# GpSimd's long instructions cut in two, and a new order of all engines' queues, in a fused attention and feed-forward kernel

## The chip, the cores and the metric

The kernel runs on one core of one Trainium2 chip. A core has five engines that work side by side and meet only at semaphores: PE (matrix products), DVE (vector work), ACT (scalar functions), POOL (GpSimd, slower vector work, and some DMA issues), and SP, which here issues DMAs. Each engine takes the instructions of its own queue strictly in order. The metric is the device time of one execution in microseconds; smaller is better.

## What is computed

Attention in which some heads see all earlier keys and the others only four "sink" keys and a window of 64, followed by a feed-forward layer with the nonlinearity h - tanh(h):

```python
scores = scale * np.matmul(q, k.transpose(0, 1, 3, 2))      # 4 x 8 heads, 768 x 768, head size 64
stream_keep = causal & (is_sink | in_win)                   # n_sink = 4, window = 64
mask = np.where(is_retrieval[head], causal, stream_keep)    # 3 of 8 heads see everything
a = softmax(np.where(mask, scores, -1e9))
x = np.matmul(a, v)                                         # as (3072, 512)
h = x @ w_in                                                # (512, 2048)
out = ((h - np.tanh(h)) @ w_out).astype(np.float32)         # (2048, 512)
```

## The kernel before

The 3072 tokens are worked on in 12 tiles of 256, three tiles for each of the four sequences. The work on one tile goes through these stages, which the kernel's operations carry as names:

- q, k and v are loaded. For tile 0 (load_first) and tile 1 (load_cast) q and k are transposed by PE. Tile 1's q and k arrive packed two rows to a partition in the buffer t16p and are copied into t16 in halves (line 714 onward, table IE says by which engine), then transposed (st_T) and copied into QK (table TE). From tile 3 on, gather copies the heads into another order: DVE works out the order of the heads (by_rank, result perm_i, L1163), POOL reads it into registers and copies q, k (L854) and v (L890) head by head, and SP issues the transposes as DMAs (turn, L756).
- st_S forms scores (PE L1373), ACT takes the exponential into pt or ptn (L1392), DVE multiplies by a mask (L1405 to L1429). st_A multiplies by v (PE L1457); keys that are far away use vf, a copy of v multiplied by each head's flag: scale_v (POOL L946) for the first two tiles, spread for the others (L909, the sink copies L918, L929). DVE normalises (L1477, L1503, L1518) and the result reaches xT by transposes.
- H_unit multiplies by w_in (PE L1604), eight pairs of 128-wide chunks for each tile; ACT takes tanh (L1618) and DVE forms h - tanh(h) in gt (L1629).
- The second product: tiles 0 to 3 use O_group (PE L1677). Tiles 4 to 11 use a seven-product scheme on 2 x 2 blocks: DVE once forms four sums of blocks of w_out (L1717), and for every tile `sums` forms four sums S of blocks of gt, each in two halves of four chunks (L1770), so eight sums of 512 columns a tile. `piece` does the seven products (PE L1803), and `take`, `fold` and `add` (L1842, L1862, L1874) put them together in PSUM evacuations on ACT, DVE or POOL. For the last tile finale_b does so in its own order. Stores go out by SP and ACT (L1663, L1894).

No engine order is found at run time. The program first lists 1653 operations, numbered as they are made, and then issues them in the order of a list of numbers, SEQ; what an engine's queue holds is the part of SEQ that belongs to it. BANK says which PSUM bank each product uses, and SIZE how many times each warm-up matmul (L2144, numbers from 128) is repeated; these fill stretches at the start in which PE would otherwise be idle. Tables of letters (A is ACT, D is DVE, P is POOL) say which engine takes an operation that more than one can do: CASTS, TE, XE, IE, OE, SUMS (eight letters a tile), ADDS, TAKES. A branch at the end repeats the work in a general form if more than three heads see everything; it is not taken here.

The numbers that matter below: 37 and 38 are the first loads of v, 57 and 58 tile 1's loads of q and k (POOL's queue); 59 and 60 are the copies of tile 1's q halves, 61 and 62 those of k; 93 is the exponential of the last head pair of tile 0; 161 is tile 1's first scores; 170 is the mask of tile 1's second head pair; 244 is perm_i; 482 and 497 are stores of early tiles and 266 to 271 the loads of tile 4 (SP); 909 to 915 are tile 4's sums; 948 is a mask on ptn in tile 7 and 952 the product that uses it; 1615 to 1622 are the last tile's sums, 1636 an add there, 1642 and 1644 the last evacuations into the output block F, 1643 and 1645 its stores.

Of the kernel before, what the change touches and what calls it, by code (L numbers as in the profile page):

```python
# [16 lines left out]

SEQ = [
# [107 lines left out]
SIZE = {128: 19, 129: 14, 130: 10, 131: 6, 132: 3, 133: 4, 134: 3}  # L126
# [262 lines left out]
def kernel(  # L389
# [12 lines left out]
    nc = tc.nc  # L402
# [1920 lines left out]
```

## Time and profile before

| | us |
|---|---|
| three runs | 225.25, 222.69, 223.52 |
| their median | 223.52 |
| the profiled execution | 224.28 |
| its span, first to last instruction | 222.5 |
| granted clock of TensorE, mean over the span | 0.998 |
| DMA queue of SP and ACT loads, share of the span of 16 engines | 58.3% |
| DMA queue of POOL's loads, the same | 30.3% |
| POOL's L1770 (the sums) | 18 instructions, medians of their three groups 1.15 to 1.16 us |

The profile is one execution taken by the hardware profiler. "PE busy" has modelled ends, since matmuls are pipelined. In rows of the timeline the columns are the start, the time, the engine, the line of the kernel, the operation, what it writes and reads with partitions x columns, the count, and in brackets the idle time before it and what ended that. In rows of groups the columns after the bar are total busy us, mean ns of one, and the idle time before with what ended it. In rows of stretches they are, after the stretch and its length, the busy time and count of PE, PEld (weight loads), DVE, ACT and POOL, then the granted clock, the DMA share and GB/s.

### The profile page before, as it was taken

How to read it: one execution, taken by the hardware profiler on the slowest of the kernel's cores; microseconds unless marked ns; L12 is line 12 of the kernel's file. 1: busy time of each engine (PE TensorE's matmuls, PEld its weight loads, DVE VectorE, ACT ScalarE, POOL GpSimd, SP SyncE). 2: the span in 40 equal slices, each digit the busy share in tenths (PEclk: the TensorE clock that was granted, in tenths of full speed). 3: DMA queues.
4: the chain of work that ended last, by engine and by line, in shares of the span. 5: the costliest groups of instructions: out<-in, count | busy, mean ns of one | idle time of the engine just before them, and what ended most of it. 6: DMA issues, size and time to landing. Idle time of an engine off the chain costs nothing.

```text
span 222.5 us, 6576 instructions
## 1 busy us (share of the span) xinstructions
PE 211.9 (95%) x2474; PEld 175.5 (79%) x2474; DVE 182.0 (82%) x468; ACT 135.0 (61%) x216; POOL 128.4 (58%) x262
## 2 busy tenths in 40 slices
PE   7969999999999999999989999999999999999990
PEld 7657788778985585968877988988889888988870
DVE  5779889476878598979999888999899786799771
ACT  3979646897275759465557759473646857356110
POOL 8785967533784571578981873774864455034400
PEclk9999999999999999999999999999999999999999
DMA  6999999997999999899989499999246031010223
GB/s 171 170 200 198 198 160 160 182 190 165 228 188 205 233 187 236 169 198 236 253 167 189 100 175 225 252 196 174 73 78 164 0 94 52 21 29 0 99 94 105
DMA packets 112743, 34.56 MB, mean 155 GB/s; under 512 B 98882, under 2 KB 112194, under 8 KB 112706
## 3 DMA queue, kind: packets, MB, share of 16 engines
q1 hardware_dynamic: 86896, 26.75, 58.3%
q0 software_dynamic: 24992, 6.82, 30.3%
q10 hardware_dynamic: 818, 0.52, 0.8%
q8 instruction: 20, 0.33, 0.6%
q14 instruction: 17, 0.14, 0.2%
HBM read 27.26 MB, written 6.29 MB: 151 GB/s over the span
## 4 chain that ended last, share of the span: by engine, by line
PE 83%; DVE 7%; DMA 4%; issue 2%; POOL 2%; ACT 1%; POOLq 0%; DVEq 0%; ACTq 0%
PE banks L1604 35%; PE banks L1803 20%; PE banks L1677 13%; PE banks L1373 7%; PE banks L1457 7%; DMA t16p<-in_k_dram 3%; DVE gt L1629 1%; DVE m L1770 1%; POOL v L673 1%; DVE ptn L1405 1%; DMA out_dram<-ot 1%; PE banks L1248 1%; DVE gu L1874 1%; DVE ot L1862 1%; DVE pt L1429 1%
## 5 line engine op out<-in xcount | busy, mean ns | idle before, releaser
L1604 PE MATMUL banks<-xT,win 128*128 128x256 f16 x768 | 95.5, 273 | 0.2 <-DVE ot L1862 0.2
L1618 ACT ACTIVATE th<-banks 128x512 f32<-128x512 f32 x96 | 54.7, 599 | 48.3 <-PE banks L1604 37.9
L1604 PEld LDWEIGHTS <-win 128*128 128x128 f16 x768 | 72.5, 98 | 10.1 <-issue 1.0
L1629 DVE SCALAR_TENSOR_TENSOR gt<-th,banks 128x512 f16<-128x512 f32 x88 | 58.1, 679 | 7.8 <-ACT th L1618 6.8
L1392 ACT ACTIVATE pt<-banks 128x1024 f16<-128x1024 f32 (+3 forms) x57 | 49.3, 905 | 13.1 <-PE banks L1373 12.1
L854 POOL CAST t<-rawqk 128x256 f16 x64 | 24.7, 412 | 17.0 <-DMA rawqk<-in_q_dram 9.1
L1803 PEld LDWEIGHTS <-m 128*128 128x128 f16 x256 | 24.4, 98 | 3.3 <-issue 0.4
L1677 PE MATMUL banks<-wout,gt 128*128 128x256 f16 (+1 forms) x160 | 25.7, 294 | 0.0
L890 POOL CAST v<-rawv 128x128 f16 x64 | 19.5, 333 | 8.0 <-DMA rawv<-in_v_dram 7.9
L1503 DVE TENSOR_TENSOR x16t<-banks,rinv 128x128 f32 (+1 forms) x80 | 22.8, 286 | 1.3
L1373 PE MATMUL banks<-QK 64*128 64x128 f16 (+1 forms) x343 | 20.8, 236 | 0.0
L1803 PEld LDWEIGHTS <-gt 128*128 128x128 f16 x192 | 18.3, 98 | 2.4 <-issue 0.3
L1373 PEld LDWEIGHTS <-QK 64*128 64x128 f16 x343 | 13.0, 94 | 7.3 <-issue 6.0
L1770 POOL TENSOR_TENSOR m<-gt 128x512 f16<-128x512 f16 x8 | 9.3, 1158 | 16.3 <-ACT th L1618 10.9
L1457 PEld LDWEIGHTS <-pt 128*128 128x128 f16 x390 | 16.1, 97 | 2.3 <-issue 1.2
L1392 ACT ACTIVATE ptn<-banks 128x1024 f16<-128x1024 f32 (+1 forms) x18 | 17.1, 952 | 1.1 <-PE banks L1373 1.0
L1677 PEld LDWEIGHTS <-gt 128*128 128x128 f16 x160 | 14.1, 98 | 4.6 <-issue 0.7
L1803 PE MATMUL banks<-wout,gt 128*128 128x256 f16 x128 | 17.7, 273 | 0.0
L1803 PE MATMUL banks<-wout,m 128*128 128x256 f16 x128 | 17.6, 273 | 0.0
L1457 PE MATMUL banks<-v,pt 128*128 128x65 f16 x208 | 16.0, 193 | 0.0
L1429 DVE TENSOR_TENSOR pt<-pt,m4r 128x1024 f16<-128x1024 f16 (+1 forms) x18 | 13.2, 733 | 2.7 <-ACT pt L1392 2.7
L1457 PE MATMUL banks<-vf,pt 128*128 128x65 f16 x182 | 13.0, 193 | 0.7 <-DVE gt L1629 0.7
(129 smaller groups left out, 309.7 us busy)
## 6 DMA issues: line engine op xcount, KB each, us to landing
rawqk<-in_q_dram SPq DMA_DIRECT2D x18, 256.0 KB, 4.3
out_dram<-ot SPq DMA_DIRECT2D x18, 256.0 KB, 2.8
rawqk<-in_k_dram SPq DMA_DIRECT2D x17, 256.0 KB, 4.2
rawv<-in_v_dram SPq DMA_DIRECT2D x16, 256.0 KB, 4.9
win<-in_moe_w_in_dram POOLq DMA_DIRECT2D x4, 512.0 KB, 8.9
wout<-in_moe_w_out_dram POOLq DMA_DIRECT2D x4, 512.0 KB, 8.4
out_dram<-ot SPq DMA_DIRECT2D x10, 128.0 KB, 3.7
v<-in_v_dram POOLq DMA_DIRECT2D x6, 128.0 KB, 7.2
```

The costliest lines, as they stand in the source:

```text
L854: nc.gpsimd.tensor_copy(out=c5()[:, :, :, s_ : s_ + 1, :], in_=r5()[:, :, :, at, :])
L890: nc.gpsimd.tensor_copy(out=v1s[b]()[:, g * NB : g * NB + NB, RANK[s_] : RANK[s_] + 1, 0:D], in_=rw()[:, :, at, :],)
L1373: nc.tensor.matmul(out=flat[:, 512 * hh + o : 512 * hh + o + nb * 128], lhsT=lhsT, rhs=QK[p_, hp, q_0 : q_0 + nb * 128], start=not added, ...
L1392: nc.scalar.activation(out=o_, in_=i_, func=AF.Exp, scale=inv_sqrt_d)
L1429: nc.vector.tensor_mul(out=pv, in0=pv, in1=m)
L1457: nc.tensor.matmul(out=av()[:, i, hh, :], lhsT=pt()[:, hh, co : co + 128], rhs=vv, start=(jb == first_jb[hh]), stop=(jb == qb),)
L1503: nc.vector.tensor_mul(out=xt()[:, :, at, :], in0=av()[:, :, hh : hh + 1, 0:D], in1=rinv()[:, :, hh : hh + 1].unsqueeze(3).to_broadcast([1 ...
L1604: nc.tensor.matmul(out=ph()[:, j, :], lhsT=w_in_t[fb // 4][:, cb, f0 : f0 + 128], rhs=xT()[:, :, cb, :], start=(cb == 0), stop=(cb == HP - 1),
L1618: lambda: nc.scalar.activation(out=th()[:], in_=ph()[:], func=AF.Tanh, scale=1.0 / XS),
L1629: nc.vector.scalar_tensor_tensor(out=o_, in0=a, scalar=-XS, in1=b, op0=ALU.mult, op1=ALU.add,)
L1677: nc.tensor.matmul(out=po()[:, c0:c1], lhsT=gt()[:, f, ts * 128 : ts * 128 + 128], rhs=w_out_t[:, f, c0:c1], start=(f == 0), stop=(f == NF ...
L1803: nc.tensor.matmul(out=po()[:, at : at + CM], lhsT=lhs(c), rhs=rhs(c), start=c == 0, stop=c == NC - 1,)
```

## The change

HALVES is 2, and a new helper, `parts`, cuts a range in two where the engine is POOL and leaves it whole otherwise. Three operations use it: the sums (two chunks of 128 columns each instead of four), the far products of scale_v (four heads each instead of eight) and the sink copies of spread (two of the four blocks each). Both halves belong to one operation of the list: the second follows the first directly on POOL's queue, and those who wait for the operation wait for the second.

SEQ, BANK, SIZE and the tables of engines are replaced. SUMS has 18 P before and 30 after; three sums go from POOL to DVE and fifteen the other way. Of ADDS, seven go from DVE to POOL and six back. Of the copies and evacuations in CASTS, TE, XE, IE, OE and TAKES, 23 change between ACT and DVE. The set of operations, what they compute and what they wait for stay.

In POOL's queue the loads at the start go from 37, 38, 57, 58 to 58, 37, 38, 57. In ACT's queue 60, 93 becomes 60, 59, 93. In DVE's queue 170 stands before 278, 174 and 175 instead of behind 174 and 175; 244 stands behind the shrink of tile 1's sixth pair (371) instead of behind 380 and 243; 948 no longer follows 914, which is POOL's; 1620 stands before 1622 and 1621, and 1617, 1605, 1612 and 1636 are POOL's. In PE's queue 981 stands ahead of 952. In SP's queue 482 and 497 stand ahead of 271 and 268.

```diff
+HALVES = 2
 SEQ = [
-    1, 4, 7, 8, 3, 5, 6, 14, 13, 10, 18, 0, 19, 9, 12, 11, 128, 20, 21, 22, 30, 31, 129, 51, 15, 35, 37,
...
+    311, 317, 307, 319, 265, 318, 320, 322, 314, 313, 482, 497, 271, 268, 507, 349, 508, 350, 361, 509,
...
+    1646, 1647, 1610, 1611, 1612, 1635, 1639, 1644, 1613, 1631, 1632, 1628, 1636, 1645, 1642, 1643,
+    1648, 1650, 1649, 1651, 1652,
 ]
...
-SIZE = {128: 19, 129: 14, 130: 10, 131: 6, 132: 3, 133: 4, 134: 3}
+SIZE = {128: 20, 129: 22, 130: 6, 131: 4}
...
+    def parts(eng, a, b):
+        n = HALVES if eng == "POOL" else 1
+        return [slice(a + (b - a) * i // n, a + (b - a) * (i + 1) // n) for i in range(n)]
...
-    TE = (('DA', 'AD', 'AD', 'DD'), ('AA', 'AA', 'AA', 'DD'), ('AD', 'DD', 'DD', 'AA'))
-    XE = ('DDAD', 'DAAD', 'DADA')
+    TE = (('AA', 'AA', 'DD', 'AA'), ('AA', 'DD', 'AA', 'DD'), ('AA', 'AA', 'DD', 'DA'))
+    XE = ('AADD', 'DAAD', 'DADA')
...
-    CASTS = ('DA', 'AA')
+    CASTS = ('DD', 'AD')
...
-    SUMS = ('DDDDDDDD', 'DDDDDDDD', 'DDDDDDDD', 'DDDDDDDD', 'DPDPDPPD', 'PDDDPDDD', 'DDDDDDDD', 'DDPDDDDD', 'DDDDDPPP', 'DPPDDDPD', 'DPDDDDPP', 'PDDDDDPD')
-    ADDS = ('PPP', 'PPP', 'PPP', 'PPP', 'DDD', 'DPP', 'PDP', 'PPP', 'PDP', 'DPD', 'PDD', 'DPP')
-    TAKES = ('AA', 'AA', 'AA', 'AA', 'AA', 'AA', 'AA', 'AA', 'AD', 'AA', 'AA', 'AA')
+    SUMS = ('DDDDDDDD', 'DDDDDDDD', 'DDDDDDDD', 'DDDDDDDD', 'DDDPPPPP', 'DDDDPDDD', 'DPPDDDPP', 'DDPPDDDP', 'PDPDPPPP', 'PPPDDDDP', 'PPDDDDPP', 'PDPDDDPD')
+    ADDS = ('PPP', 'PPP', 'PPP', 'PPP', 'DDP', 'PDD', 'PDD', 'PDP', 'DPD', 'PPD', 'PPP', 'PPP')
+    TAKES = ('AA', 'AA', 'AA', 'AA', 'AA', 'AA', 'AD', 'AA', 'AD', 'AD', 'AA', 'AA')
...
-    IE = (('DA', 'DA'), ('DA', 'DA'))
+    IE = (('AA', 'DD'), ('DA', 'DA'))
...
-    OE = ('AADA', 'DDDA', 'AAAA', 'AAAA', 'AAAA', 'AAAA', 'AAAA')
+    OE = ('AAAD', 'DADA', 'AAAA', 'AAAA', 'AAAA', 'AAAA', 'AAAA')
...
-                    lambda: nc.gpsimd.tensor_copy(
-                        out=vfs[b]()[0:64, :, NGEN:H, :],
...
+                    lambda: [
+                        nc.gpsimd.tensor_copy(
+                            out=vfs[b]()[0:64, x, NGEN:H, :],
...
+                        for x in parts("POOL", 0, 4)
+                    ],
...
-                    lambda jb=jb, fl=fl, eng=eng: engs[eng].tensor_mul(
-                        out=vfs[b]()[:, jb, :, :], in0=v1s[b]()[:, jb, :, :],
...
+                        engs[eng].tensor_mul(
+                            out=vfs[b]()[:, jb, x, :], in0=v1s[b]()[:, jb, x, :],
+                            in1=fl[:, x].unsqueeze(2).to_broadcast([128, x.stop - x.start, D + 1]),
+                        )
+                        for x in parts(eng, 0, H)
...
-                        lambda k=k, fn=fn, a=a, b=b, cs=cs, e=e: getattr(engs[e], fn)(
-                            out=S4[k][:, cs, :], in0=a()[:, cs, :], in1=b()[:, cs, :]
-                        ),
+                        lambda k=k, fn=fn, a=a, b=b, cs=cs, e=e: [
+                            getattr(engs[e], fn)(
+                                out=S4[k][:, x, :], in0=a()[:, x, :], in1=b()[:, x, :]
+                            )
+                            for x in parts(e, cs.start, cs.stop)
+                        ],
```

More of the change, by code (lines that the diff above doesn't have):

```diff
@@ L917, in spread @@
                     "POOL", 1290,
-                    lambda: nc.gpsimd.tensor_copy(
-                        out=vfs[b]()[0:64, :, NGEN:H, :],
-                        in_=v1s[b]()[0:64, 0, NGEN:H, :].unsqueeze(1).to_broadcast(
-                            [64, 4, H - NGEN, D + 1]
-                        ),
-                    ),
+                    lambda: [
+                        nc.gpsimd.tensor_copy(
+                            out=vfs[b]()[0:64, x, NGEN:H, :],
+                            in_=v1s[b]()[0:64, 0, NGEN:H, :].unsqueeze(1).to_broadcast(
+                                [64, x.stop - x.start, H - NGEN, D + 1]
+                            ),
+                        )
+                        for x in parts("POOL", 0, 4)
+                    ],
                     r=[("v1", b, 0, 1)] + after, w=[("vf", b, "low")],
@@ L945, in scale_v @@
                     eng, cost[eng],
-                    lambda jb=jb, fl=fl, eng=eng: engs[eng].tensor_mul(
-                        out=vfs[b]()[:, jb, :, :], in0=v1s[b]()[:, jb, :, :],
-                        in1=fl[:].unsqueeze(2).to_broadcast([128, H, D + 1]),
-                    ),
+                    lambda jb=jb, fl=fl, eng=eng: [
+                        engs[eng].tensor_mul(
[4 more added lines that the diff above has]
+                    ],
                     r=[("v1", b, jb, 0), ("v1", b, jb, 1), "rflag0", "rflag"],
@@ L1769, in sums @@
                         e, cost[e],
-                        lambda k=k, fn=fn, a=a, b=b, cs=cs, e=e: getattr(engs[e], fn)(
-                            out=S4[k][:, cs, :], in0=a()[:, cs, :], in1=b()[:, cs, :]
-                        ),
+                        lambda k=k, fn=fn, a=a, b=b, cs=cs, e=e: [
+                            getattr(engs[e], fn)(
+                                out=S4[k][:, x, :], in0=a()[:, x, :], in1=b()[:, x, :]
+                            )
+                            for x in parts(e, cs.start, cs.stop)
+                        ],
                         r=g_[h * NFU // SH : (h + 1) * NFU // SH] + [("S", x, h) for x in r],
```

204 rows, old and new, of tables (BANK, SEQ) are left out of this document.

## The prediction, made before the changed kernel had run

> **What bounds the kernel now.** I read the page first (busy shares), then the stretches, then what PE waited for, then the chain, then single rows.
>
> ```profile
> PE 211.9 (95%) x2474; PEld 175.5 (79%) x2474; DVE 182.0 (82%) x468; ACT 135.0 (61%) x216; POOL 128.4 (58%) x262
> ```
> ```profile
> 40.00:60.00 20.00, 20.00 (x296) 16.44 (x295) 12.83 (x41) 14.87 (x22) 9.25 (x26) 1.00 1.15 191
> 100.00:120.00 20.00, 19.09 (x217) 15.96 (x215) 19.55 (x47) 12.10 (x20) 15.96 (x30) 1.00 0.97 214
> ```
> ```profile
> PE banks L1457 <- DVE ptn L1405: 0.9, 1, 0.9
> PE banks L1457 <- DVE gt L1629: 0.7, 1, 0.7
> ```
>
> PE has work 95% of the time, all of the 20 us from 40 to 60, at the full granted clock (the 1.00 after POOL's share). Between 100 and 120 DVE is busy 19.55 of 20 and PE falls to 19.09. The matrix work is the same after the change: nothing is added to PE, and its warm-up matmuls fall from 59 to 52 repeats (the sums of SIZE), which run where PE would wait anyway and so cost nothing. So a new order can win only what PE loses now: the opening before the dense part, 0.7 us at 22, 0.9 us at 113, and the end after the last matmul. Everything that only makes DVE, ACT or POOL freer is worth nothing beyond that.
>
> **The lock that the halves act on.** Three times a DVE instruction stands far beyond its usual time, and each time a long GpSimd instruction began beside it:
>
> ```profile
> 12.05 1.48 DVE L1230 COPY t<-t16p 128x512 f16<-128x512 f16 x1 [1.18 <-DMA t16p<-in_k_dram]
> 12.30 1.06 POOL L946 TENSOR_TENSOR vf<-v,rflag 128x520 f16<-128x520 f16 x1
> 20.62 1.47 DVE L1429 TENSOR_TENSOR pt<-pt,m 128x1024 f16<-128x1024 f16 x1
> 20.50 1.04 POOL L946 TENSOR_TENSOR vf<-v,rflag 128x520 f16<-128x520 f16 x1
> 111.86 1.51 DVE L1405 TENSOR_TENSOR ptn<-ptn,mS 128x768 f16<-128x768 f16 x1
> 111.76 1.19 POOL L1770 TENSOR_TENSOR m<-gt 128x512 f16<-128x512 f16 x1
> 112.90 0.67 POOL L879 COPY kc<-QK 128x192 f16<-128x192 f16 x1
> 102.66 0.55 DVE L1405 TENSOR_TENSOR ptn<-ptn,mS 128x768 f16<-128x768 f16 x1
> ```
>
> The same mask on ptn takes 0.55 undisturbed and 1.51 behind a sum: 0.96 lost. It ends 0.42 after the sum does, while POOL's next copy is drawn out: DVE gets in between two POOL instructions. That is what a half offers. [...]
>
> **Part 1: what a half costs.**
>
> ```profile
> L1770 POOL TENSOR_TENSOR m<-gt 128x512 f16<-128x512 f16 x8 | 9.3, 1158 | 16.3 <-ACT th L1618 10.9 <-DVE gt L1629 4.6 <-PE banks L1803 0.9
> L909 POOL TENSOR_TENSOR vf<-v,rflagr 128x195 f16<-128x195 f16 x12 | 6.1, 514 | 0.2
> L1874 POOL TENSOR_TENSOR ot<-gu,ot 128x256 f32<-128x256 f32 x8 | 5.8, 731 | 9.0 <-ACT th L1618 3.7 <-ACT gu L1842 2.2 <-DVE ot L1862 2.2
> L946 POOL TENSOR_TENSOR vf<-v,rflag 128x520 f16<-128x520 f16 x4 | 4.2, 1052 | 4.7 <-DMA v<-in_v_dram 3.5 <-DVE rflag L1067 1.2
> L918 POOL COPY vf<-v 64x1300 f16<-64x1300 f16 x3 | 3.8, 1281 | 0.0
> L929 POOL COPY vf<-v 64x650 f16<-64x650 f16 x3 | 2.2, 727 | 0.2
> ```
>
> No sum of 256 columns is in the trace. L909 and L946 give (1052-514)/325 = 1.66 ns a column, so 256 columns are 0.61; L1874 does 256 with two full inputs, as the sums have, in 0.73. I take 0.73 (same count, same kind of inputs) and keep 0.61 to 0.73. Two halves are then 1.46 for a sum that was 1.16, +0.30; +0.19 for each of the four far products (2 x 0.62 - 1.05) and +0.17 for each of the three sink copies (2 x 0.727 - 1.28). SUMS has 18 P now and 30 after, so POOL's sums go from 18 x 1.16 = 20.9 to 30 x 1.46 = 43.8 us. With +0.8 and +0.5 for the others, and one more add (0.73), POOL's 128.4 becomes about 153 of 222 us: hidden under PE on the whole, and priced below where it may not be. DVE loses 12 sums (0.42 to 0.49 each) and one add, 5 to 6 us; PE does not wait for most of them, so this is worth 0 outside the places named here. The net of the lock is small: POOL's long sums hold it twice as long in total for half as long each time.
>
> **Part 2: the opening.** PE's dense part begins with the first matmuls of H at 16.49.
>
> ```profile
> t16p<-in_q_dram POOLq DMA_DIRECT2D x1, 256.0 KB, 4.8
> t16p<-in_k_dram POOLq DMA_DIRECT2D x1, 256.0 KB, 6.1
> 10.58 0.61 ACT L1228 COPY t<-t16p 128x512 f16<-128x512 f16 x1
> 11.11 0.81 ACT L1392 ACTIVATE pt<-banks 128x768 f16<-128x768 f32 x1
> 13.91 0.76 ACT L1228 COPY QK<-banks 128x256 f16<-128x256 f16 x2 [1.25 <-PE banks L1248]
> 14.80 0.77 ACT L1228 COPY QK<-banks 128x256 f16<-128x256 f16 x2
> 16.49 1.91 PE L1604 MATMUL banks<-xT,win 128*128 128x256 f16 x16
> ```
>
> Now k is the fourth load of POOL's queue and lands at 12.0; DVE's copy of it stands ahead of everything DVE does next and, held by a far product, ends only at 13.53. After: k goes first, then two v, then q, so q takes the place that lands at about 12.0. Both q copies are ACT's (IE 'AA'), ahead of the exponential of the last head pair of tile 0: 12.05 + 2 x 0.61 + 0.81 = 14.1, against 11.92 now. Then four copies by ACT (five run from 13.91 to 15.57 now, so four take 1.33) to 15.4, scores of tile 1 (0.5) to 15.9, transposes (0.33), dense part at 16.2. The 0.33 is an estimate from PE's pace in that row (1.91 for 16). Gain 0.3. If q lands 0.4 sooner, 0.7; if it slips by 1 us, a loss of 0.7. I take -0.3, since the sum of loads ahead of q is that ahead of k now.
>
> **Part 3: the two waits.** At 22 the mask that PE waited for (the 1.47) stands two short DVE instructions earlier, and a far product holds DVE at most 0.62 instead of 1.04: -0.7 (bounds -0.7 and 0). At 113 the mask no longer follows one of tile 4's sums (0.34 to the next start), a sum holds DVE 0.73 instead of 1.19, and PE has one more chunk of H (four matmuls of 0.12, the same pace) ahead of the wait: 0.34 + 0.46 + 0.48 covers the 0.9, but DVE's queue there is full, so I take -0.7 (bounds -0.9 and 0).
>
> **Part 4: the end.**
>
> ```profile
> 207.21 1.15 POOL L1770 TENSOR_TENSOR m<-gt 128x512 f16<-128x512 f16 x1 [1.62 <-DVE gt L1629]
> 214.81 0.42 DVE L1862 SCALAR_TENSOR_TENSOR ot<-banks,gu 128x256 f32<-128x256 f32 x1 [1.29 <-PE banks L1803]
> 215.16 0.41 DVE L1770 TENSOR_TENSOR m<-gt,m 128x512 f16<-128x512 f16 x1
> 215.49 0.42 DVE L1874 TENSOR_TENSOR ot<-ot,ot 128x256 f32<-128x256 f32 x1
> 215.82 0.42 DVE L1862 SCALAR_TENSOR_TENSOR gu<-banks,ot 128x256 f32<-128x256 f32 x1
> 216.94 1.79 DMA out_dram<-ot
> ```
>
> DVE runs eight instructions in a row here, one each 0.34. After, the sum is done earlier and the add is POOL's, so two go: 0.68 at most; the store that closes the chain, of F, then waits for its other half, one place later. I take -0.35 (bounds -0.65 and +0.5). The cover: POOL's last queue is three split sums and four adds, 3 x 1.46 + 4 x 0.73 = 7.3 from about 207.2, done at 214.5, where its add is wanted at 215.5; beyond 1 us of slip it costs directly.
>
> **Part 5: moves with a cover.** The head order (perm) is formed by DVE later; POOL's gather of tile 3 starts from it.
>
> ```profile
> 32.02 0.17 DVE L1163 TENSOR_SCALAR perm_i<-pos_a 128x8 int32<-128x8 f32 x1
> 38.66 0.69 DVE L1629 SCALAR_TENSOR_TENSOR gt<-th,banks 128x512 f16<-128x512 f32 x1 [0.28 <-ACT th L1618]
> 37.40 0.40 POOL L854 COPY t<-rawqk 128x256 f16 x1 [1.21 <-DVE mS L1230]
> QK<-t SPq DMA_TRANSPOSE x2, 5.3
> 51.70 0.51 PE L1373 MATMUL banks<-QK 64*128 64x256 f16 x10
> ```
>
> It now stands right behind the shrink that ended at 39.35 (tile 1, sixth pair). With 0.9 for POOL's reading of the order (an estimate, bounded above by the 5.4 between perm and the first copy now), eight copies of 0.40 end at 43.6 and SP's transposes 5.3 later, at 49; wanted at 51.7, or about 50 if PE is 1.5 ahead. Nothing, or +1 if the cover goes. SP's queue gets two stores ahead of tile 4's loads; both wait for evacuations that now end before 47, when those loads are issued anyway. Switches of copies and evacuations between ACT and DVE (23 in all) are 0.3 to 0.6 us each, outside the opening all beside PE's work: 0.
>
> **Part 6: new waits.** From 23 to 214 us this order has waits of 0.9 and little else. A new order has its own: I take +0.9, the same again (bounds 0, and +4.6 as in the slower rival).
>
> **The sum:** -0.3 - 0.7 - 0.7 - 0.35 + 0.9 = -1.15 against the profiled execution, 224.28 (span 222.5 and 1.8 around it): 223.1. That execution is 0.76 above the median of the three runs, 223.52, so for a median I give 222.4, 0.5% faster. About 1% is what this measurement can tell from no change; the three runs alone spread by 2.6 us.
>
> **Rivals.**
> *Slower: POOL becomes late at tiles 4 and 8.*
>
> ```profile
> sum 18.00, PE 17.09 PEld 13.07 DVE 16.88 ACT 10.48 POOL 15.29; mean PE 5.70 PEld 4.36 DVE 5.63 ACT 3.50 POOL 5.10
> L879 POOL COPY kc<-QK 128x192 f16<-128x192 f16 x12 | 5.2, 440 | 4.4 <-DMA QK<-t 4.3
> ```
>
> From 96 to 114 (the row's sum) POOL is busy 15.3 of 18.0. Five split sums (7.3) replace four of 1.16 (4.6): 18.0 of 18.0, unless something slides out of the stretch. The copy L879 that DVE cut into took 0.67 against a mean of 0.44, so a hand-over costs POOL 0.23 or more. Ten halves with one each are 2.3 more, and as soon as the other work cannot slide by that much, PE waits for the second and third sums: 2.3 at tile 4 and 2.3 at tile 8 (six sums on POOL), less the 2.05 of parts 2 to 4: 223.5 + 4.6 - 2.05 = 226.1. Against it: POOL's copies for later tiles do stand there and can slide. [...]
> *No change of note:* the 0.9 and 0.7 come back elsewhere and ACT's q copies eat the opening: 223.5.
> *Faster:* no new waits and the better bounds: -0.7 - 0.7 - 0.9 - 0.65 = -2.95 from the median, 220.6.
>
> **How the numbers follow.** Forecast 0.47 (its own range 220.9 to 224.0), no change of note 0.18, slower 0.20, faster 0.15. Of the forecast 0.08 falls under 221.3. So faster by over 1% 0.23, within 1% 0.57, slower 0.20. The range 220.2 to 226.0 leaves out about half of the two outer cases.
>
> **What would show it.** Right: dense part at 15.8 to 16.3; no DVE instruction over 1.2 us beside a sum; sums of 256 columns at 0.61 to 0.73; two DVE rows fewer after 214. Wrong: q landing after 12.5 with ACT idle before it, POOL busy all 18 us between 96 and 114 with PE waiting for m, or new PE waits above 2 us in sum between 23 and 214.

## The result, and the profile after

| | before | after |
|---|---|---|
| median of 4 runs, us | 224.21 (222.69 to 225.25) | 233.43 (232.89 to 236.51) |
| ratio to before, 95% interval | | 1.041 (1.032 to 1.050) |
| the profiled execution, us | 224.28 | 232.89 |
| its span, us | 222.5 | 231.2 |
| granted clock over the span | 0.998 | 0.987 |

The change makes the kernel 4% slower. Forecast was 222.4 us, in 220.2 to 226.0. The run of 236.51 us lies more than 1.5% above the fastest of its kernel and is left out of the ratio. Line numbers are 6 to 15 higher in the changed kernel: the sums stand at L1783, H at L1616, the pieces at L1818, h - tanh(h) at L1641.

Busy shares and what PE waited for, of the kernel after (page, view of PE's waits):

```profile
PE 215.5 (93%) x2467; PEld 175.8 (76%) x2467; DVE 184.8 (80%) x454; ACT 135.4 (59%) x217; POOL 156.1 (68%) x312
```
```profile
PE banks L1996 <- DVE ot L1990: 3.2, 1, 3.2
PE banks L1469 <- DVE pt L1441: 1.6, 1, 1.6
PE banks L1818 <- POOL m L1783: 1.4, 2, 0.8
PE banks L1385 <- DVE gt L1641: 1.4, 1, 1.4
PE banks L1818 <- DVE m L1783: 1.2, 1, 1.2
PE banks L1818 <- DVE x16t L1515: 0.6, 1, 0.6
```

The first row is the wait at the very end, 2.6 before. Before, the list between opening and end held only two waits worth a row; now there are six single waits of 0.6 to 1.6 us, on DVE and on POOL. They fall in a few stretches (columns as before: length, busy time of PE, PEld, DVE, ACT, POOL, then granted clock):

```profile
100.00:120.00 20.00, 19.52 (x228) 16.46 (x228) 18.55 (x46) 12.34 (x21) 15.59 (x34) 1.00 1.10 199
140.00:160.00 20.00, 16.78 (x195) 14.15 (x192) 18.93 (x36) 8.06 (x14) 17.86 (x39) 1.00 0.85 153
160.00:180.00 20.00, 19.65 (x211) 16.43 (x211) 15.90 (x38) 10.49 (x17) 17.28 (x36) 0.91 0.31 73
```

From 140 to 160 DVE and POOL are both nearly full (18.93 and 17.86 of 20) and PE loses 3.2 us; from 160 the clock itself is below full. Where the time goes is best seen by PE's progress: the start of the n-th matmul of H in the two profiles, read from PE's rows (the orders place H a little differently, which moves a single entry by up to 1.5 us, and two executions of the changed kernel, this one and f4 below, differ by as much in single entries).

```
n-th H matmul      1st    129th   289th   321st   385th   449th   513th   545th   737th   span
before, us        16.49   58.46   93.28  100.94  121.85  135.28  149.33  157.62  200.55  222.5
after, us         15.97   57.42   92.86  102.38  121.99  136.25  152.48  164.20  207.54  231.2
after - before    -0.5    -1.0    -0.4    +1.4    +0.1    +1.0    +3.2    +6.6    +7.0    +8.7
```

The new order is ahead by 1 us until 58 us, and gains about 1 again near 113 (+1.4 to +0.1). It loses in three places above all: some 2 us around 100, 5 to 6 us between 140 and 164, and 1.7 at the end. In sum: -1.0 to 58 us, +8.0 from there to 207, +1.7 behind.

**Around 100 us** (rows of the timeline, after):

```profile
93.59 2.19 DVE L1729 TENSOR_TENSOR gu<-wout 128x256 f16<-128x256 f16 x1
93.59 0.29 POOL L896 CAST v<-rawv 128x128 f16 x1
93.83 2.21 POOL L860 CAST t<-rawqk 128x256 f16 x6
96.74 0.60 ACT L1630 ACTIVATE th<-banks 128x512 f32<-128x512 f32 x1 [2.54 <-DVE gt L1641]
100.48 0.66 PE L1385 MATMUL banks<-QK 64*128 64x256 f16 x14 [1.35 <-DVE gt L1641]
```

One of DVE's sums of blocks of w_out (operation 858) takes 2.19 us; at 93.09 in the kernel before it took 0.39. It is held through a whole row of gather copies on POOL. gt comes late, ACT idles 2.54, and the scores behind wait 1.35.

**From 144 to 164 us:**

```profile
144.64 0.83 POOL L875 COPY kc<-QK 128x768 f16<-128x768 f16 x1 [1.59 <-DMA QK<-t]
146.24 1.40 POOL L925 COPY vf<-v 64x650 f16<-64x650 f16 x2
147.60 1.29 POOL L1783 TENSOR_TENSOR m<-gt,m 128x256 f16<-128x256 f16 x2
149.69 1.63 POOL L1783 TENSOR_TENSOR m<-gt,m 128x256 f16<-128x256 f16 x2
150.41 0.39 PE L1818 MATMUL banks<-wout,m 128*128 128x256 f16 x2 [0.81 <-POOL m L1783]
151.38 0.39 PE L1818 MATMUL banks<-wout,m 128*128 128x256 f16 x2 [0.58 <-POOL m L1783]
```
```profile
154.32 3.01 DVE L1783 TENSOR_TENSOR m<-gt 128x512 f16<-128x512 f16 x1
154.50 2.54 POOL L1783 TENSOR_TENSOR m<-m,gt 128x256 f16<-128x256 f16 x4
158.76 0.61 DVE L1441 TENSOR_TENSOR pt<-pt,m4r 128x768 f16<-128x768 f16 x1
159.43 0.36 PE L1469 MATMUL banks<-v,pt 128*128 128x65 f16 x6 [1.61 <-DVE pt L1441]
```
```profile
156.98:160.39 3.41, 1.23 (x15) 0.80 (x14) 3.37 (x10) 0.60 (x1) 2.86 (x7) 1.00 1.00 239
160.39:163.81 3.42, 3.42 (x17) 2.37 (x17) 2.84 (x8) 1.19 (x2) 3.42 (x12) 0.50 0.21 70
```

Tile 6's last two sums are POOL's now and stand behind a copy that waited 1.59 us for a DMA and behind a sink copy of 1.40. They end at 148.89 and 151.32; the kernel before had them on DVE, done at 138.0 and 142.4. PE waits twice, for the two halves of the second of these sums: the first half ends at 150.35 (149.69 and 0.66) and PE starts at 150.41. So a reader starts on the half that it needs, and does not wait for both as the text on the change had it. Then one DVE sum, which takes 0.41 alone, is held for 3.01 us through four halves of POOL; the mask behind it is late and PE waits 1.61, then 0.57 more. After these waits the granted clock is 0.50 for 3.4 us: 1.7 us of PE's full pace.

**The end:**

```profile
215.15 0.68 DVE L1641 SCALAR_TENSOR_TENSOR gt<-th,banks 128x512 f16<-128x512 f32 x1
218.93 1.76 DVE L1783 TENSOR_TENSOR m<-gt 128x512 f16<-128x512 f16 x2
219.56 1.66 POOL L1783 TENSOR_TENSOR m<-gt,m 128x256 f16<-128x256 f16 x2
220.74 0.61 PE L1818 MATMUL banks<-gu,m 128*128 128x256 f16 x4 [1.25 <-DVE m L1783]
228.06 0.16 PE L1996 MATMUL banks<-ot 1*2 1x2 f16 x1 [3.22 <-DVE ot L1990]
```

The last gt ends at 215.83 and the piece that needs the sums made from it could start at 219.5, 3.7 us later; before, it was 207.7 and 213.7, 6.0 us. In the new order the last H products stand closer to the pieces. The sums, drawn out by POOL's halves beside them (two take 1.76, and one alone 0.41), no longer fit in. Of the 1.7 us, 1.25 are this wait; the other part is the very end, 3.22 against 2.55 before.

### The profile page after: what moved, and what is told of

It is laid out like the page before. It is cut to its first block, busy times and chain, and to the rows that moved or that the text cites. A ratio compares the mean times of both kernels' runs of the same rounds, so it can differ in the third digit from the quotient of the medians.

```text
span 231.2 us, 6608 instructions
## 1 busy us (share of the span) xinstructions
PE 215.5 (93%) x2467; PEld 175.8 (76%) x2467; DVE 184.8 (80%) x454; ACT 135.4 (59%) x217; POOL 156.1 (68%) x312
## 5 line engine op out<-in xcount | busy, mean ns | idle before, releaser
L1616 PE MATMUL banks<-xT,win 128*128 128x256 f16 x768 | 97.1, 273 | 0.8 <-DVE gt L1641 0.4
L1616 PEld LDWEIGHTS <-win 128*128 128x128 f16 x768 | 72.3, 98 | 12.0 <-issue 1.9
L1641 DVE SCALAR_TENSOR_TENSOR gt<-th,banks 128x512 f16<-128x512 f32 x88 | 58.1, 680 | 8.2 <-ACT th L1630 6.5
L860 POOL CAST t<-rawqk 128x256 f16 x64 | 25.4, 426 | 9.7 <-DMA rawqk<-in_k_dram 4.6
L896 POOL CAST v<-rawv 128x128 f16 x64 | 21.5, 368 | 14.3 <-DMA rawv<-in_v_dram 14.2
L1818 PEld LDWEIGHTS <-m 128*128 128x128 f16 x256 | 24.6, 99 | 6.8 <-POOL m L1783 1.9
L1783 POOL TENSOR_TENSOR m<-gt 128x256 f16<-128x256 f16 x24 | 16.9, 724 | 12.2 <-DVE gt L1641 8.9
L1818 PEld LDWEIGHTS <-gt 128*128 128x128 f16 x192 | 18.7, 100 | 3.8 <-issue 1.0
L1818 PE MATMUL banks<-wout,gt 128*128 128x256 f16 x128 | 18.8, 282 | 0.6 <-DVE x16t L1515 0.6
L1818 PE MATMUL banks<-wout,m 128*128 128x256 f16 x128 | 17.9, 273 | 1.4 <-POOL m L1783 1.4
L1689 PEld LDWEIGHTS <-gt 128*128 128x128 f16 x160 | 14.3, 98 | 5.1 <-issue 0.9
L1783 POOL TENSOR_TENSOR m<-gt,m 128x256 f16<-128x256 f16 x22 | 15.6, 729 | 2.7 <-DVE m L1783 2.7
L1441 DVE TENSOR_TENSOR pt<-pt,m4r 128x1024 f16<-128x1024 f16 (+1 forms) x18 | 15.2, 846 | 2.1 <-ACT pt L1404 2.1
## 6 DMA issues: line engine op xcount, KB each, us to landing
win<-in_moe_w_in_dram POOLq DMA_DIRECT2D x4, 512.0 KB, 10.5
```

Of the source, the lines that this page charges most:

```text
L860: nc.gpsimd.tensor_copy(out=c5()[:, :, :, s_ : s_ + 1, :], in_=r5()[:, :, :, at, :])
L896: nc.gpsimd.tensor_copy(out=v1s[b]()[:, g * NB : g * NB + NB, RANK[s_] : RANK[s_] + 1, 0:D], in_=rw()[:, :, at, :],)
L1616: nc.tensor.matmul(out=ph()[:, j, :], lhsT=w_in_t[fb // 4][:, cb, f0 : f0 + 128], rhs=xT()[:, :, cb, :], start=(cb == 0), stop=(cb == HP - 1),
L1641: nc.vector.scalar_tensor_tensor(out=o_, in0=a, scalar=-XS, in1=b, op0=ALU.mult, op1=ALU.add,)
L1689: nc.tensor.matmul(out=po()[:, c0:c1], lhsT=gt()[:, f, ts * 128 : ts * 128 + 128], rhs=w_out_t[:, f, c0:c1], start=(f == 0), stop=(f == NF ...
L1783: getattr(engs[e], fn)(out=S4[k][:, x, :], in0=a()[:, x, :], in1=b()[:, x, :])
```

## The experiments

**Halves or order.** Each of the four kernels takes one half of the change. `e1_whole` sets HALVES to 1 in the changed kernel:

```diff
-HALVES = 2
+HALVES = 1
```

> The changed kernel with HALVES = 1: its order and its engines, every long GpSimd instruction whole again. Theory H (the halves cost the time: pairs of halves take 1.30 instead of 1.15 us and hold DVE as long as a whole sum or longer): the waits at 149 to 151 us and the 3.01 us sum of DVE at 154 shrink, 225 to 228 us. Theory T (thirty sums on GpSimd in place of eighteen, whole or cut): GpSimd loses only some 30 x 0.14 = 4 us of its 156, DVE is still held for about three whole instructions at 154; 230 to 234 us. Theory O (the order of the queues): no change, 232 to 235 us.

Measured: 1.042 (1.034 to 1.051) times the kernel before; the changed kernel itself is at 1.041. `e2_halves_old` is the kernel before (SEQ, BANK, SIZE, all tables) with the helper `parts` and HALVES = 2.

> The kernel before, its order and its engines, with the halves alone. Theory H: slower than the kernel before by 2 us or more, 226 to 230 us. Theories T and O: 223 to 225 us, as before; the mask at 112 us falls from 1.51 to about 1 us, which is worth at most the 0.9 us that PE waits there.

Measured: 0.999 (0.997 to 1.001). Rows of e2, where the kernel before had 1.51 and 0.9:

```profile
111.78 1.02 DVE L1417 TENSOR_TENSOR ptn<-ptn,mS 128x768 f16<-128x768 f16 x1
112.86 0.24 PE L1469 MATMUL banks<-v,ptn 128*128 128x65 f16 x2 [0.43 <-DVE ptn L1417]
```

So the halves shorten the hold at this place as the prediction said (the wait falls from 0.9 to 0.43), and in the time they neither cost nor win anything that can be measured; whole or cut, the new order is 4% slower. Theory H is out.

`e3_new_order_old_eng` and `e4_old_order_new_eng` cross SEQ and the tables:

```diff
     # e3: SEQ, BANK, SIZE after; e4: SEQ, BANK, SIZE before
-    TE, XE, CASTS, SUMS, ADDS, TAKES, IE, OE of the one
+    TE, XE, CASTS, SUMS, ADDS, TAKES, IE, OE of the other
```

> The changed kernel's order of operations with the kernel before's tables of engines (18 sums on GpSimd, the old adds, copies and evacuations), halves kept. Theory T: most of the loss goes, 224 to 228 us. Theories H and O: 230 us or more. The order was not made for these tables, so up to 2 us of other waits may come in either way, in the opening above all.

> The kernel before's order of operations with the changed kernel's tables of engines (30 sums on GpSimd), halves kept. Theory T: 228 us or more, with PE waiting for GpSimd's sums. Theory O: 223 to 227 us. Theory H: 228 us or more. The old order was not made for these tables, so up to 2 us of other waits may come in.

Measured: 1.090 (1.086 to 1.094) and 1.047 (1.043 to 1.052). Theory T wanted e3 fast, theory O wanted e4 fast, and both are slow, e3 by far more than the changed kernel: with its own tables the new order loses 4%, with the old ones 9%, so crossing an order with other tables says little about either. T and O stay undivided here.

**Which sums.** `f1_four_back` moves four sums of the changed kernel to DVE, `h2_tile6` and `h3_tile7` two each, `f2_old_sums` takes the whole old table:

```diff
     # tiles 6 and 7 of SUMS (f1: both lines, h2: tile 6, h3: tile 7)
-    'DPPDDDPP', 'DDPPDDDP',
+    'DPPDDDDD', 'DDDDDDDP',
```

> The changed kernel with four of its thirty GpSimd sums back on DVE: the last two of tile 6 (for which PE waits at 149.4 and 150.9 us) and the two of tile 7 whose four halves hold DVE's sum for 3.01 us at 154.3. Theory late (GpSimd comes to these sums some 8 us after their inputs, and its unbroken row of halves keeps DVE from the mask at 157): the three waits of 0.99, 0.76 and 1.77 us go, and with the last of them the stretch of lower granted clock behind it: 227.5 to 230 us. Theory full (DVE has no room for four more sums of 0.42 us there): the waits move to DVE's sums and masks, 231.5 to 234.5 us.

> The changed kernel with the kernel before's eighteen sums on GpSimd and all else as changed: its order, its adds, copies and evacuations. Theory late: 226 to 230 us, the waits between 140 and 165 us gone and the one at 219 us smaller. Theory order (the new order makes the waits, whoever forms the sums): 231 us or more.

> The changed kernel with only tile 6's last two sums back on DVE. If late sums cost most: the waits at 149 and 151 us go and 2 us or more of the 3.5 that four sums brought, 230.5 to 231.5 us; the four halves of tile 7 still follow one another, and DVE's sum there takes 2.5 to 3.0 us. If the lock-out costs most: 232 to 233.5 us, the wait for the mask at 157 to 160 us still 1.6 us.

> The changed kernel with only tile 7's two sums back on DVE, so that the row of four halves is gone. If the lock-out costs most: the wait at 157 to 160 us goes, 230 to 231.5 us. If late sums cost most: the waits at 149 and 151 us stay at 0.6 to 1.0 each, 231.5 to 233 us.

Measured, times before: f1 1.030 (1.024 to 1.037), f2 1.040 (1.035 to 1.044), h2 1.022 (1.018 to 1.027), h3 1.036 (1.029 to 1.044). h2 takes 1.9 of the 4.1%, about 4 us, and more than late sums alone were expected to bring; all four letters in f1 bring 1.1%, and the intervals of the two overlap, so a figure for each letter can't be given. In the profiles of both, the waits at 150, 151 and 159 us are gone, and smaller ones of 0.4 to 0.5 come at 143, 144 and 159. h3's time (median 231.26) lies where the lock-out theory put it (230 to 231.5), but it can't be told from the changed kernel by its interval; in its profile the wait for the mask is gone, those for tile 6's sums stay at 0.6 and 0.2, and one of 0.8 comes at 164 us. In h2 the same four halves still follow one another:

```profile
154.09 3.10 POOL L1783 TENSOR_TENSOR m<-m,gt 128x256 f16<-128x256 f16 x4 [1.75 <-DVE m L1783]
154.46 1.40 DVE L1783 TENSOR_TENSOR m<-gt 128x512 f16<-128x512 f16 x2
155.78 0.88 DVE L1889 TENSOR_TENSOR ot<-gu,ot 128x256 f32<-128x256 f32 x1
```

Here POOL is early enough to wait 1.75 for DVE, and DVE gets in after each half: its two sums take 1.40 together. In h2, then, undoing POOL's lateness undid the lock-out as well, though its row of halves is the same. The number of sums on POOL alone is not the cause either: f2 has 18 as before and is as slow, with 2.0 us of waits for DVE's sums in its list (its table belongs to another order, as in e3, and may cost by that).

Is the 3.01 chance? `f4_again` is the changed kernel once more, and `h4_cast_between` puts a gather copy between the two sums:

```diff
     # h4, in SEQ
-    1154, 1292, 1291, 1279, 1277,
+    1154, 1292, 1279, 1291, 1277,
```

> The changed kernel unaltered, profiled once more. If it is settled by the order that DVE's sum at 154.3 us is held through four halves of GpSimd, the 3.01 us return, within 0.2. If it hangs on a few tenths of a us in how the two engines meet, that row takes 0.4 to 1.1 us now or another row of DVE is held instead, and the time stays within 232.5 to 234.5 us only if the late sums, not this one, set it.

> The changed kernel with one of GpSimd's gather copies (operation 1279) put between the two sums of tile 7, so that the row is half, half, cast, half, half. If any unbroken row of GpSimd keeps DVE out once it has missed its turn: the same DVE sum takes 2.6 to 3.4 us again, the same time, 232 to 234 us. If it is the sums that follow one another without a new wait of GpSimd: DVE gets in at the cast or before, the row takes 2 us or less, the wait for the mask falls by 1 us or more, 231 to 232.5 us.

f4: 232.67 us in its one run. h4: 1.043 (1.036 to 1.050). Rows of f4 and its two stretches around the wait, then rows of h4:

```profile
155.58 3.00 DVE L1783 TENSOR_TENSOR m<-gt 128x512 f16<-128x512 f16 x1
160.68 0.35 PE L1469 MATMUL banks<-v,pt 128*128 128x65 f16 x6 [1.64 <-DVE pt L1441]
```
```profile
156.20:159.62 3.42, 2.85 (x29) 2.32 (x27) 3.42 (x4) 0.00 (x0) 3.42 (x7) 1.00 0.75 108
159.62:163.03 3.41, 1.77 (x20) 1.53 (x21) 3.31 (x12) 1.03 (x2) 2.51 (x9) 1.00 1.04 276
```
```profile
156.01 3.24 DVE L1783 TENSOR_TENSOR m<-gt 128x512 f16<-128x512 f16 x1
156.18 1.29 POOL L1783 TENSOR_TENSOR m<-m,gt 128x256 f16<-128x256 f16 x2
157.42 0.28 POOL L896 CAST v<-rawv 128x128 f16 x1
157.67 1.29 POOL L1783 TENSOR_TENSOR m<-m,gt 128x256 f16<-128x256 f16 x2
```

The lock-out returns to 0.01 us, and one cast more makes it 0.24 longer: a row with a cast in it does it as well. The clock of f4, after the same wait, stays full; with 232.67 us it is hardly faster for it, so the drop is not what makes the kernel slow.

**The held row at 94 us.** `g1_moved` is f1 with operation 858 set right behind 853. `g3_until_134` has the new order and its tables for the first 1064 operations and the old ones behind; `g4_until_134_moved` is g3 with 858 moved.

```diff
-    853, 720, 732, 733, 734, 820, 808, 809, 838, 743, 744, 839, 840, 745, 780, 781, 799, 821, 822, 746,
-    747, 800, 841, 801, 823, 858, 692, 693, 695, 690, 691, 696, 697, 708, 640, 639, 756, 754, 694, 761,
+    853, 858, 720, 732, 733, 734, 820, 808, 809, 838, 743, 744, 839, 840, 745, 780, 781, 799, 821, 822,
+    746, 747, 800, 841, 801, 823, 692, 693, 695, 690, 691, 696, 697, 708, 640, 639, 756, 754, 694, 761,
```

> The kernel with four sums back on DVE (229.91 us), and in the order one more edit: operation 858, the last sum of blocks of w_out (DVE, held for 2.2 to 2.7 us behind seven or eight gather copies of GpSimd in every run of the new order, at 94 us), stands right behind 853, five us earlier. Theory held (this one row makes gt late and PE's scores wait 1.3 to 1.8 us at 100 us): the wait falls under 0.5 us and the time by 1.0 to 1.8 us, to 228.1 to 228.9 us. Theory full (DVE's queue is as late without it, another instruction being held in its place): the wait stays over 1 us, 229.5 to 230.5 us.

> The changed kernel's order and engines for its first 1064 operations (to 134 us), the kernel before's for all the rest, halves kept. By the progress of the H matmuls the new order is 1.0 to 2.5 us behind at 135 us, 5.4 us more are lost from 145 to 162, and 1.7 at the end. Theory places (three places of the new order lose, each by itself): 224.0 to 226.0 us. Theory debt (work pushed back before 134 us, GpSimd's gather copies above all, is what is missing later, whatever the order there): 228 us or more.

> The run before with operation 858 moved behind 853. Theory held: the wait at 100 us goes here too, 1.0 to 1.8 us less than the run before: 222.5 to 224.5 us, at best 0.4% faster than the kernel before (the opening's 0.6 to 1.0 us). Theory full: the same as the run before.

Measured: g1 1.020 (1.013 to 1.027), 228.09 us against 229.91 of f1; g3 1.013 (1.006 to 1.020), 226.94; g4 1.004 (1.000 to 1.008), 225.32. Rows of g1:

```profile
88.18 0.68 DVE L1729 TENSOR_TENSOR gu<-wout 128x256 f16<-128x256 f16 x3
98.98 0.67 PE L1385 MATMUL banks<-QK 64*128 64x256 f16 x15
```

Three such sums now take 0.68 together and the scores start without a wait. The two pairs give -1.8 and -1.6 us. g3 and g4 stay 0.9 and 0.8 us above what was expected of them, so the first 134 us lose a little more than the one wait. Each pair's intervals overlap, but in every profile of the new order with 858 in its place the row took 2.2 to 2.7 us, and it is gone in all three kernels that move it (g1, g4, and g2 below): theory held, by the trace. g3, 1 us from theory places and more from theory debt, says that what comes behind 134 us loses by its own order, for the most part.

**Opening and end.** `f3_opening` has the new order only for its first 224 operations, the old one behind; `g2_old_end` is g1 with the old order behind operation 1503 of the list, `h1_new_end` the old order with the new one behind 1540.

```diff
     # f3; g2 and h1 are joined in the same way
-SEQ = after
+SEQ = after[:224] + [i for i in before if i not in after[:224]]
```

> The changed kernel's order and engines for its first 224 operations (to some 29 us), and the kernel before's order and engines for all the rest; halves kept. If the gains of the opening are gains of their own: dense part at 16.0, the wait at 21 us 0.4, that at 112 us 0.4 as with the halves alone, so 222.0 to 223.0 us, 0.3 to 0.7% faster than before. If what PE wins at the start is lost where it next waits for DVE or a load: 223.3 to 224 us, the same as before. If the seam between the two orders makes a wait of its own: above 224 us, with the wait between 25 and 45 us.

> As the run with operation 858 moved, and behind the first 1503 operations (203 us) the kernel before's order and engines: the last tile's third sum and first add, two adds and a sum of tile 10 on DVE again. If the end of the new order is a loss of its own (wait of 1.25 us at 220 for the last tile's sums, 3.2 us instead of 2.6 at the very end): 1.5 to 2.2 us less than that run. If the end is late only because DVE and GpSimd come to it late from earlier tiles: within 0.5 us of it.

> The kernel before's order and engines for the first 1540 operations (to 202 us), the changed kernel's for the rest; halves kept. Theory end (the new order's end loses by itself): a wait of about 1.2 us for the last tile's sums and 3.2 us instead of 2.5 at the very end, 1.5 to 2.2 us slower than the kernel before: 225.0 to 225.7 us. Theory late (the end is late only from what comes before): 223.0 to 224.2 us.

Measured: f3 0.999 (0.996 to 1.002), h1 1.011 (1.006 to 1.016), g2 1.017 (1.011 to 1.022), 227.58 us against 228.09 of g1. In its profile f3 is 1.0 us ahead of the kernel before at the 321st H matmul and stays so to the end, but against e2, whose halves alone gain 0.05 there, runs that spread by 2 us show nothing. h1 loses 2.6 us of median, a little more than either theory had; rows of h1:

```profile
213.64 0.61 PE L1818 MATMUL banks<-gu,m 128*128 128x256 f16 x4 [1.21 <-DVE m L1783]
220.99 0.16 PE L1996 MATMUL banks<-ot 1*2 1x2 f16 x1 [3.25 <-DVE ot L1990]
```

The same two waits as in the changed kernel, with 1.0 us more of waits at the seam (200 us). So the end loses by itself, 1.6 us if the seam's waits are taken off. g2 won only 0.5, which by its time alone is the other theory's figure: its end is the old one (2.49 at the very end, no wait at 216), but the seam made 1.6 us of waits from 196 to 202. With tile 6's and 7's sums back, 858 moved and the old end, g2 is still 1.7% slower. No version that was run beats the kernel before: e2 and f3 equal it.

## Why the prediction was wrong

**What came as forecast.** q landed at 12.0, the dense part began at 15.97 (forecast 16.2, said right at 15.8 to 16.3), and by the 129th H matmul PE was 1.0 us ahead, the sum of parts 2 and 3 (-0.3 and -0.7), though measured as -0.5 at the start of the dense part and -0.5 at the wait at 22 us (0.7 before, 0.2 after). That this fits so well is partly luck: of the kernels with the old opening, h1 reaches that matmul at 57.53 and e2 at 58.20, against 58.46 before and 57.42 after, so executions alone differ by as much as 0.7. The wait at 113 went. Two rows of DVE fewer stand after the last pieces, but the very end got longer all the same. POOL is busy 156.1 us (forecast about 153).

```profile
12.00 1.14 ACT L1240 COPY t<-t16p 128x512 f16<-128x512 f16 x2 [0.20 <-DMA t16p<-in_q_dram]
15.97 1.91 PE L1616 MATMUL banks<-xT,win 128*128 128x256 f16 x16
```
```profile
L1783 POOL TENSOR_TENSOR m<-gt 128x256 f16<-128x256 f16 x24 | 16.9, 724 | 12.2 <-DVE gt L1641 8.9 <-PE banks L1818 2.4 <-PE banks L1616 0.7
```

A half of 256 columns takes 0.724 in the mean, the 0.73 that was taken, and a pair 1.44 against the forecast 1.46. That is again luck in part: the mean holds halves that DVE drew out. Where nothing cuts in, a half takes 0.66 to 0.67 (42 of the 60) and a pair 1.29 to 1.30, so the split itself costs +0.14 and not +0.30.

Two of the prediction's own signs told against it: a DVE instruction over 1.2 us beside a sum (the 3.01), and new PE waits above 2 us between 23 and 214 (5.8 in sum, small ones included).

**The step that failed** is part 6: "From 23 to 214 us this order has waits of 0.9 and little else. A new order has its own: I take +0.9, the same again (bounds 0, and +4.6 ...)". It measured about +8 even with the wait won at 113 taken off, nearly twice its upper bound: PE goes from 1.0 us ahead at 58 us to 7.0 behind at 207. The 0.9 was no estimate of this order's queues; it took the record of the old order as the price of any. Two sentences stood behind it. One is "hidden under PE on the whole", from POOL's share of 153 in 222 us: a share says nothing of what stands ahead of a sum in POOL's queue, and that was a copy waiting for a DMA (tile 6: 1.4 us of waits, and with what followed from them some 4 us by h2). The other is "DVE gets in between two POOL instructions", read from a single meeting: in most meetings it does (383 of 417, counted below), but not at 93.59 (1.6 to 1.8 us) and not at 154.32 (1.61 and, in that profile, 1.7 of lower clock). The profile before holds the counterexample:

```profile
147.53 1.63 DVE L1874 TENSOR_TENSOR gu<-gu 128x256 f32<-128x256 f32 x1
147.34 0.72 POOL L1874 TENSOR_TENSOR ot<-gu,ot 128x256 f32<-128x256 f32 x1
148.01 0.39 POOL L854 CAST t<-rawqk 128x256 f16 x1
148.37 0.51 POOL L909 TENSOR_TENSOR vf<-v,rflagr 128x195 f16<-128x195 f16 x1
```

An add of DVE that takes 0.41 alone ends only at 149.16, behind three POOL instructions in a row. Nor were there three long holds only, as the prediction counted: a mask at 103.22 took 1.42 as well, beside a sum.

Rival "POOL becomes late" had the sign and a late POOL, but by a POOL without a gap, at the wrong tiles (4 and 8, where PE waits for none of POOL's sums) and with half the price: from 96 to 114 POOL is busy 12.9 us, not 18.0.

**Part 4** had the wrong sign: -0.35 forecast (bounds -0.65 and +0.5), +1.7 measured, 1.6 by h1. It counted DVE's instructions and POOL's cover, and did not follow PE's queue, in which the last H products come closer to the pieces that need their sums (the wait of 1.25). Why the very end takes 0.7 longer with two DVE rows fewer was not tested.

**What stays open.** Small waits between 55 and 90 us (0.2 us in this profile, up to 1.4 in others of the new order) and from 120 to 145 (0.5) were not undone one by one; g4, which still has those before 134, is at most 0.8% slower than before. PE's idle time after 16 us rises by 6.2 us (4.3 to 10.5) and the clock costs 1.7; about 1.3 of the loss is in no wait that the rows show. The gains of the edits don't add up either (h2 alone is as fast as f1 or faster), and 1.7% remain in g2, some 1.6 us of it the seam's.

## What to carry to other kernels

Price a reordered queue by following each moved piece to what now stands ahead of it, DMA waits included; the old order's waits say nothing about the new one's. Cutting a long GpSimd instruction in two mostly let DVE in at the cut (383 of 417 meetings here were over at the first change of instruction); but in a row of GpSimd that doesn't pause, DVE was at times kept out for longer (34 of 303 meetings, in e1 through ten instructions), so keep urgent DVE work out of the way of such rows. And an order and its table of engines are best changed together: the new order under the old tables was 9% slower, under its own 4%.

## What the runs showed of the hardware that was not expected

**DVE is kept out of whole rows.** DVE and POOL do not meet only at semaphores: in e1 an add that takes 0.41 alone took 4.21 us, through ten instructions on POOL:

```profile
153.08 4.21 DVE L1889 TENSOR_TENSOR gu<-gu 128x256 f32<-128x256 f32 x1
```

Counted over all 18 profiles, DMA issues left out: 417 times a DVE instruction ran 0.12 us or more over the shortest of its shape and had begun while POOL was in an instruction that another followed within 0.06 us. In 383 the surplus was over within 0.15 us of the first change of instruction; in 34 it was not (24 if 0.25 us are allowed), and ten of the 34 are operation 858. Of the 114 cases in which POOL had paused just ahead of the instruction it was in, none is among the 34. The 34 are all TENSOR_TENSOR with both inputs in SBUF (masks, sums, adds, blocks of w_out). It was thus seen only in a running row, but 269 of the 303 meetings with a running row also ended at the first change. What decides among those is open. The 1.51 behind a whole sum and the 1.02 in e2 were over with one sum or half; the holds of 2 to 4 us are longer than any one instruction of POOL there (1.14 at most in the row of e1).

**The clock fell after one wait and not after its twin.** After the changed kernel's wait of 1.61 us it was 0.50 for 3.41 us; after the 1.64 us of f4, 1.78 of e1 and 1.82 of h4 it stayed at 1.00. In the profiles before and after, the clock stayed full for 215.04, 153.60 and 64.85 us at a time: 63, 45 and 19 times the 3.413 us of the drop. Cut into stretches of that length, counted back from the last change of the clock, PE is busy 36% of the stretch ahead of the drop (1.23 us, the row at 156.98), with both waits in it; in f4 the waits lie in two stretches, with PE busy 83% and 52% (2.85 and 1.77 us, its rows above). In the profiles before and after, of the stretches at full clock from 8 us on, the three with PE busy 36%, 5% and 5% were followed by half the clock, and all others, with 54% or more, by the full clock. So where the waits fell in these stretches went with the drop here, and their length did not; that such stretches decide is the author's reading of these profiles.
